# Four of the filling matmul groups at the front of a recurrence-and-convolution kernel take other forms

## The chip, the cores and the metric

The kernel runs on one core of one Trainium2 chip. The metric is the device time of one execution in microseconds (us); less is better. Engines are named as in the profile: PE (TensorE), DVE (VectorE), ACT (ScalarE), POOL (GpSimd), SP (SyncE, which here only issues DMAs). "PEld" is PE's weight loading, which can overlap its matmuls.

## What is computed

Two blocks follow each other on x of shape (4, 6272, 256), batch, sequence, channels. The first is a gated recurrence along the sequence. The second projects its result to three parts, convolves one part circularly along the whole sequence with a long filter, multiplies by the two other parts and projects again:

```python
f = lower_bound + (1 - lower_bound) * sigmoid(f_logit)
h[t] = f[t] * h[t-1] + (1 - f[t]) * x[t]          # y = h, per batch and channel
x1, x2, x3 = split(y @ w_proj, 3)
conv = irfft(rfft(x2, axis=1) * rfft(filter_fft, axis=0), axis=1)
out = (x1 * conv * x3) @ w_out
```

## The kernel before, in words

The sequence of 6272 is treated as 128 x 49, and the long convolution is done by discrete Fourier transforms written as matmuls with tables. The kernel first makes the tables and the filter's spectrum (`prepare`), and then handles the four batches one after the other: the recurrence in 13 chunks of 512 steps (`hgrn`), the projection of the middle part (`phase_p`), the transforms in 16 units (`phase_f1`, `mini`, `unit`), the two other parts (`gate`), and the inverse transform, product and last projection (`phase_o`). Parts of the next batch's recurrence are woven between these.

Nothing of this order is found at run time. Each piece of work is registered as an operation with `op(...)`, numbered as it is registered, and the long string `ORDER` lists number, engine and a PSUM bank for each; `emit` issues them in that order. Each engine works off its own instructions in order and waits where data or a buffer isn't ready. An operation with `take` gets the bank of the list as its argument `p`; `PS` is the whole PSUM, 8 banks of 512 float32 columns on 128 partitions.

The filling groups are the 24 operations "warm" (line 597). Each issues four float16 matmuls of the identity tile with itself, read as float16: 128 rows, 128 weight columns, 256 moving columns. Nobody reads what they write. In the list's order of PE the first eight are the groups 20, 3, 7, 12, 13, 4, 15, 8, all with bank 0, ahead of every other matmul. Two more come later in the front (behind rotation 5), three in the middle of the run, eleven in the tail.

The work of the front, as far as the prediction follows it:

- Loads of the filter: 13 groups of 512 KB (the last is smaller) on SP's queue (line 619) into ten raw buffers. Groups 10, 11 and 12 reuse the first three. Behind them on the same queue come the loads of f_logit and x.
- A cast of each group from the raw buffer into one of two buffers `afs` (lines 284, 296, 289: the helper `copy` on ACT, POOL or DVE). Group 0 is cast on ACT, 1 to 5, 7, 9 and 8 on POOL, 6 on ACT, 10 to 12 on DVE. A cast into a buffer waits for the rotation that read it two groups before.
- A rotation of each group on PE: four matmuls with float32 weights and 256 columns (line 630), into two PSUM banks. Rotation 0 has banks 0 and 1, rotation 1 has 2 and 3, and so on around.
- Two casts of each rotation's result into `f` (ACT, line 284, some on DVE, line 289). ACT's first of these stands behind the sine tables of line 560, which wait for DVE.
- When all groups are there, the filter's two transforms: line 655 and line 673.
- The recurrence: transposes in row pairs, float32, 64 rows each (line 349), the gate (lines 362, 364) and the scan on DVE (line 370).

Later forms that the prediction uses as prices: line 398 and line 714 (projections, float16), line 727 and 790 and 743 (forward transforms), line 832 (inverse, 98 rows), line 895 (64 rows in pairs, float16), line 913 (last projection, float32).

Of the kernel before, what the change touches and what calls it, by code (L numbers as in the profile page):

```python
# [33 lines left out]
NK = 3  # L34
NO = 2
WARM = 24
NEP = 128
UE = 8
NU = NEP // UE
MARGIN = 1.0  # L40
# [20 lines left out]
class Plan:  # L61
# [14 lines left out]
    def op(self, kind, cost, fn, r=(), w=(), dma=0.0, lag=0.0, table=None, take=0, src=None, part=None, margin=0.0):  # L76
        preds = set()
        for t in r:
            if t in self.writer:
                preds.add(self.writer[t])  # L80
        for t in w:
            if t in self.writer:
                preds.add(self.writer[t])
            preds.update(self.readers.get(t, ()))
        me = len(self.ops)
        if src is not None:
            preds.add(src)
            self.ops[src]["users"].append(me)
        self.ops.append(dict(kind=kind, batch=self.batch, cost=cost, fn=fn, preds=preds, dma=dma, lag=lag,
                             table=table, take=take, src=src, part=part, margin=margin, users=[]))  # L90
        for t in r:
            self.readers.setdefault(t, set()).add(me)
        for t in w:
            self.writer[t] = me
            self.readers[t] = set()
        return me
# [98 lines left out]
def kernel(  # L195
# [10 lines left out]
    nc = tc.nc  # L206
# [4 lines left out]
    op = plan.op  # L211

    konst = ctx.enter_context(tc.tile_pool(name="konst", bufs=1))
    iden = konst.tile([128, 128], F32, name="iden")
# [21 lines left out]

    X2 = konst.tile([128, NEP * PW + 16], F16, name="X2")
    xv = X2[:, 0:NEP * PW].rearrange("m (i c) -> m i c", c=PW)

# [17 lines left out]
    PS = psp.tile([128, 8, 512], F32, name="PS")  # L257

    def Wr(kh):

        return [("W", kh, i) for i in range(3)]
# [174 lines left out]
    def prepare(head, tmp):  # L436
# [11 lines left out]
        cols = tmp.tile([128, 16], F32, name="cols")  # L448
# [7 lines left out]
        for i in range(2):  # L456
            small(lambda e, i=i: dve.tensor_copy(rot[:, i * 128:(i + 1) * 128], iden[:]), 128,
                  r=["iden"], w=["rot"], kind="turns")
# [16 lines left out]
        for kh in range(2):  # L475
# [4 lines left out]
               r=["om"] + Wr(1), w=["W13"])  # L480
            for p in range(2):
# [4 lines left out]
                   r=["om"] + Wr(1), w=["W2"])  # L486
# [5 lines left out]
        w = scr[:, 2016:4080].bitcast(F32)  # L492
# [65 lines left out]
        for i, (fn, a, b, c) in enumerate(((args0, 0, 520, 4.2), (args1, 520, 1032, 4.25))):  # L558
# [3 lines left out]
               w=[f"v{i}", "sin"], table="sin")  # L562
# [3 lines left out]
        for i in range(2):  # L566
            small(lambda e, i=i: dve.tensor_scalar(FTr[:, i, 0:TB], in0=tt[i], scalar1=low,
                                                   scalar2=None, op0=AOP.mult), 98, r=["v0"],
                  w=["FTr"], kind="tabs")
            small(lambda e, i=i: pool.tensor_scalar(FTr[:, i, TB:], in0=tt[i][:, 0:Q], scalar1=low,  # L570
                                                    scalar2=None, op0=AOP.mult), 49, r=["v0"],
                  w=["FTs"], e="POOL", kind="tabs")
# [23 lines left out]

        def warm(e, p, i):
            half = iden[:].bitcast(F16)
            for k in range(4):
                nc.tensor.matmul(PS[:, p, 0:256], half[:, 0:128], half, start=True, stop=True)  # L600
        for i in range(WARM):
            op("warm", {"PE": 0.435}, lambda e, p, i=i: warm(e, p, i), r=["iden"], take=1)

        f2 = [pool_.tile([128, NEP // 2 * PF + 16], F32R, name=f"f2{p}")
              for p, pool_ in enumerate((head, tmp))]

        def gaps(e):
            for f in f2:
                pool.tensor_copy(f[:, 0:NEP // 2 * PF].rearrange("m (i c) -> m i c", c=PF)[:, :, Q:64],
                                 iden[:, 0:15].unsqueeze(1).broadcast_to([128, NEP // 2, 15]))  # L610
                pool.tensor_copy(f[:, NEP // 2 * PF:], iden[:, 0:16])
# [4 lines left out]
        for g, r0 in enumerate(range(0, Q, 4)):  # L616
# [9 lines left out]
               r=et, w=[("af", g % 2, 0), ("af", g % 2, 1)])  # L626
# [6 lines left out]
            for p in range(2):  # L633
# [4 lines left out]
                   r=["f2e"], w=[("f2", g, p)], src=rt)  # L638
        op("pad", {"POOL": 2.0}, lambda e: nc.gpsimd.memset(
            X2[:, 0:NEP * PW].rearrange("m (i c) -> m i c", c=PW)[:, :, Q:64], 0.0),  # L640
           w=[("raw", i) for i in range(7)] + [("x2", g) for g in range(NX2)] + ["Hm"])
# [6 lines left out]
        for u in range(NU):  # L648
            af = afs[:, u % 2]
            for h in range(2):  # L650

                def first(e, pb, f=f2[u // 8], j=u % 8 * UE + h * 4):
                    pa = PS[:, pb:pb + 2].rearrange("m a (i c) -> m (a i) c", c=256)
                    for i in range(4):
# [3 lines left out]
                        r=[("f2", g, u // 8) for g in range(13)] + ["D1r", "f2e"],  # L658
                        w=[("FF1", u, h)], take=2)
# [6 lines left out]
                r=[("af", u % 2, 0), ("af", u % 2, 1)],  # L666
                w=["mX"], e="POOL", kind="mX")

            def second(e, pb, af=af):
                for r in range(2):  # L670
                    for e2 in range(2):
# [4 lines left out]
                      r=[("af", u % 2, 0), ("af", u % 2, 1), "FTr", "FTs"], w=[("FF2", u)], take=2)  # L676
# [3 lines left out]
               r=rt, w=ht[u % 2], src=f2nd)  # L680
            for i, (p0, n, to) in enumerate(((0, M, 0), (M - TB, 64, M)) if u % 2 else ()):
                op("hst", {"SP": 0.36}, lambda e, pair=pair, u=u, p0=p0, n=n, to=to: nc.sync.dma_start(
                    H[u // 2][:, to:to + n].rearrange("j r k -> r j k"), pair[p0:p0 + n]),
                   r=ht[0] + ht[1], w=[("H", u - 1, i), ("H", u, i)], dma=0.77 if i else 1.2, lag=1.7)

        def last(e, pb):
# [11 lines left out]
           w=["Hm"], src=lst)  # L698
# [231 lines left out]
    with tc.manual_schedule():  # L930
        scopes = [ctx.enter_context(ExitStack()) for _ in range(2)]
        prepare(*(c.enter_context(tc.tile_pool(name=f"tmp{i}", bufs=1, side=side))
                  for i, (c, side) in enumerate(zip(scopes, ("right", "left")))))
        for i, t in enumerate(more_t):
# [62 lines left out]
```

## Time and profile before

| | |
|---|---|
| median of 3 runs | 457.7 us (456.73 to 458.09) |
| profiled execution, from its first to its last instruction (span) | 455.6 us |
| median less span | 2.1 us |
| mean granted clock of TensorE over the span | 0.989 |
| instructions | 14635 |
| moved by DMA | 120.74 MB, mean 265 GB/s |

The profiled execution has no time of its own besides its span; the span leaves out the little that lies ahead of the first and behind the last instruction. In the rows that follow, a start and a length are given in us, then the engine, the line of the kernel, the operation, what it writes and reads, and how many like it were merged in the row. In brackets stands how long the engine was idle ahead of the row and what released it. Lengths of matmuls overlap, since they are pipelined; what one costs in a dense row is the distance of starts.

### The profile page before, as it was taken

What the parts mean: (1) busy time and instruction counts of PE and PEld (TensorE: products, weight loads), DVE (VectorE), ACT (ScalarE), POOL (GpSimd) and SP (SyncE); (2) the same over time, 40 slices, a digit from 0 to 9 for tenths busy, and PEclk for the clock granted to TensorE, in tenths of its full rate; (3) what the DMA queues carried; (4) which work ended last, traced back from release to release, by engine and by line L of the source; (5) the groups of instructions that cost most, each with busy time, mean ns of one, the idle gap of its engine ahead of it and who ended that gap; (6) DMA issues with size and microseconds to landing.
All of it is one profiled execution on the core that took longest, in us unless ns stands there. A gap on an engine that the chain in (4) does not pass through costs nothing.

```text
span 455.6 us, 14635 instructions
## 1 busy us (share of the span) xinstructions
PE 439.6 (96%) x6009; PEld 348.4 (76%) x6009; DVE 407.4 (89%) x476; ACT 402.3 (88%) x577; POOL 308.8 (68%) x279
## 2 busy tenths in 40 slices
PE   7899999999999999999999999999999999999998
PEld 5687778677767888777668888777778896776797
DVE  8899997799999996999999977999999976989873
ACT  5899999899999987899989998999989858987563
POOL 8888973878899542788995626899994405696400
PEclk9599999999999999999999999999999999999999
DMA  8999999767898985479776896778759721765186
GB/s 326 387 371 345 378 375 361 279 187 233 299 300 282 340 300 237 169 232 374 253 264 219 285 315 272 237 250 303 261 177 317 301 95 46 248 187 185 47 321 246
DMA packets 44434, 120.74 MB, mean 265 GB/s; under 512 B 4304, under 2 KB 7632, under 8 KB 44368
## 3 DMA queue, kind: packets, MB, share of 16 engines
q1 hardware_dynamic: 44368, 119.82, 74.5%
q8 instruction: 47, 0.77, 0.7%
q14 instruction: 19, 0.16, 0.1%
HBM read 86.12 MB, written 31.98 MB: 259 GB/s over the span
## 4 chain that ended last, share of the span: by engine, by line
PE 72%; DVE 11%; ACT 9%; issue 4%; DMA 3%; POOL 1%; SPq 0%; ACTq 0%; DVEq 0%; POOLq 0%
PE PS L398 17%; PE PS L714 9%; PE PS L832 9%; PE PS L913 8%; PE PS L790 7%; DVE HA L370 7%; PE PS L727 6%; PE PS L349 6%; PE PS L895 4%; ACT fTs L362 2%; DMA X<-in_moe_filter_fft_dram 2%; PE PS L600 2%; ACT HA L284 2%; DVE ys L901 1%; ACT X L284 1%
## 5 line engine op out<-in xcount | busy, mean ns | idle before, releaser
L337 POOL TENSOR_TENSOR XT<-XT,FL 128x1024 f32<-128x1024 f32 (+1 forms) x49 | 109.9, 2247 | 55.7 <-ACT FL L335 38.5
L370 DVE TENSOR_TENSOR_SCAN HA<-fTs,HA,PS 128x512 f16<-128x512 f32 (+1 forms) x96 | 112.7, 1202 | 2.0 <-ACT fTs L362 1.1
L398 PE MATMUL PS<-HA,W 128*128 128x490 f16 (+1 forms) x416 | 100.2, 367 | 0.3 <-ACT Th L284 0.2
L822 POOL TENSOR_TENSOR PP<-HA,Hu 98x1008 f16<-98x1008 f16 x42 | 88.0, 2106 | 5.6 <-ACT HA L284 2.6
L284 ACT CAST HA<-PS 128x1024 f16<-128x1024 f32 (+1 forms) x101 | 81.2, 831 | 3.3 <-POOL PP L822 0.8
L901 DVE TENSOR_TENSOR ys<-PS,zt 128x1024 fp32r<-128x1024 f32 (+1 forms) x52 | 58.3, 1151 | 14.0 <-PE PS L895 10.3
L813 DVE TENSOR_TENSOR PP<-PS,Hu 98x1008 f16<-98x1008 f32 x54 | 63.6, 1199 | 1.5 <-PE PS L790 0.7
L362 ACT ACTIVATE fTs<-PS,nomc 128x512 f32<-128x512 f32 (+1 forms) x90 | 59.5, 680 | 4.5 <-PE PS L349 4.2
L398 PEld LDWEIGHTS <-W 128*128 128x128 f16 x416 | 35.3, 97 | 30.2 <-issue 2.9
L428 POOL TENSOR_TENSOR zt<-XS 128x490 f16<-128x490 f32 (+1 forms) x26 | 31.8, 1223 | 39.0 <-DVE ys L901 27.4
L913 PE MATMUL PS<-Wo,ys 128*128 128x256 f32 x392 | 57.5, 293 | 0.4 <-DVE ys L901 0.3
L286 ACT ACTIVATE XS<-PS 128x490 f32<-128x490 f32 (+1 forms) x88 | 51.0, 590 | 6.8 <-DVE zt L419 2.6
L832 PEld LDWEIGHTS <-PP 98*128 98x128 f16 x1024 | 49.2, 98 | 10.1 <-POOL PP L795 1.3
L284 ACT CAST Th<-PS 128x784 f16<-128x784 f32 x63 | 52.0, 828 | 3.4 <-PE PS L832 2.7
L913 PEld LDWEIGHTS PS<-Wo,ys 128*128 128x128 f32 x392 | 49.6, 188 | 4.5 <-DVE ys L901 1.2
L832 PE MATMUL PS<-VA,PP 98*128 98x98 f16 x512 | 52.1, 207 | 0.2 <-POOL PP L795 0.2
L832 PE MATMUL PS<-VB,PP 98*128 98x98 f16 x512 | 51.8, 207 | 0.0
L419 DVE TENSOR_TENSOR zt<-PS,XS 128x490 f16<-128x490 f32 (+1 forms) x78 | 49.2, 648 | 2.7 <-ACT XS L286 0.8
L335 ACT ACTIVATE FL<-FL 128x1024 f32<-128x1024 f32 (+1 forms) x49 | 49.8, 1022 | 0.6 <-DMA FL<-in_f_logit_dram 0.6
L714 PE MATMUL PS<-W,HA 128*128 128x256 f16 x392 | 44.6, 273 | 1.1 <-ACT X L284 1.1
L714 PEld LDWEIGHTS <-HA 128*128 128x128 f16 x392 | 42.9, 142 | 2.0 <-issue 1.3
L349 PE MATMUL PS<-iden,FL 64*128 64x64 f32 x736 | 41.7, 229 | 2.6 <-ACT PP L286 0.6
(119 smaller groups left out, 778.7 us busy)
## 6 DMA issues: line engine op xcount, KB each, us to landing
FL<-in_f_logit_dram SPq DMA_DIRECT2D x45, 512.0 KB, 5.3
XT<-in_x_dram SPq DMA_DIRECT2D x45, 512.0 KB, 6.2
Hu<-H SPq DMA_DIRECT2D x39, 512.0 KB, 4.6
out_dram<-osb SPq DMA_DIRECT2D x24, 512.0 KB, 4.6
out_dram<-PP SPq DMA_DIRECT2D x16, 512.0 KB, 4.8
Hl<-H SPq DMA_DIRECT2D x13, 512.0 KB, 4.7
X<-in_moe_filter_fft_dram SPq DMA_DIRECT2D x9, 512.0 KB, 7.0
out_dram<-HA SPq DMA_DIRECT2D x8, 512.0 KB, 5.7
```

What stands on the lines that cost most here:

```text
L284: nc.scalar.copy(dst, src)
L337: op("u", {"POOL": 0.1 + 0.553 * nb}, lambda e, xt=xt, ft=ft: nc.gpsimd.tensor_tensor(xt, xt, ft, op=AOP.mult), r=[("ft", k)], w=[("xt", k)])
L349: nc.tensor.transpose(bank(pb)[:, at[p] + j:at[p] + hn:nb], src[ps, j, cols], iden[ps, ps])
L362: nc.scalar.activation(fT, sT, AF.Identity, scale=by, bias=1.0)
L370: nc.vector.tensor_tensor_scan(h, fT, bank(pb)[:, 512 - hn:512 + hn], init, op0=AOP.mult, op1=AOP.add),
L398: nc.tensor.matmul(PS[:, p, 0:n], W13[:, kh, js], HA[:, HB[kh] + t0:HB[kh] + t0 + n], start=(kh == 0), stop=(kh == 1))
L714: nc.tensor.matmul(pp[:, r - r0, :], column(HB[kh], q_of(r)), W2[:, kh, :], start=(kh == 0), stop=(kh == 1))
L813: nc.vector.tensor_tensor(pr, px.unsqueeze(1).broadcast_to([TB, 2, UE, 63]), hh(), op=AOP.mult)
L822: nc.gpsimd.tensor_tensor(pr, spec[:, o, :, 1:64].unsqueeze(1).broadcast_to([TB, 2, UE, 63]), hh(), op=AOP.mult)
L832: nc.tensor.matmul(PS[:, ib + o, pr * TB:(pr + 1) * TB], PP[:TB, k, o, n, 2 * pr:2 * pr + 2, :], v[:TB], start=(n == 0), stop=(n == 1))
L901: nc.vector.tensor_tensor(late["ys"][:, yk, :, 0:rn * 128], PS[:, cb:cb + 2, 0:rn * 128], late["zt"][:].rearrange("p k r m -> p k (r m)") ...
L913: nc.tensor.matmul(po[:, i, :], late["ys"][:, yk, kh, i * 128:(i + 1) * 128], Wo[:, kh, :], start=(kh == 0), stop=(kh == 1))
```

## The change

The four filling groups 13, 4, 15 and 8, the last four of the eight ahead of all other matmuls, no longer issue four float16 matmuls of 256 columns each. Group 13 issues 48 float32 transposes of 64 rows in pairs, which write with strides of 4, 1 and 2. Group 4 issues 24 transposes of 32 rows and 16 of 64 rows into 64 columns. Group 15 issues 16 transposes of 128 rows (eight contiguous, eight at stride 4) and 16 float16 matmuls of 64 rows and 64 columns. Group 8 issues 16 float16 matmuls of 64 rows and 128 columns, 8 of 98 rows and 98 columns, and 8 of 128 rows and 128 columns. These four may write to up to four banks from bank 0 on (`take=4`, where `take` only says that a bank is passed). The list `ORDER` and the twenty other groups stay.

```diff
@@ -34,6 +34,7 @@
 WARM = 24
+FORMS = (13, 4, 15, 8)
 NEP = 128
...
         def warm(e, p, i):
             half = iden[:].bitcast(F16)
-            for k in range(4):
-                nc.tensor.matmul(PS[:, p, 0:256], half[:, 0:128], half, start=True, stop=True)
+            lo, hi = slice(0, 64), slice(64, 128)
+
+            def pairs(n, step, tiles=(lo, hi), cols=((0, 128),)):
+                for k in range(n):
+                    for c, (c0, c1) in enumerate(cols):
+                        for j, ps in enumerate(tiles):
+                            w = ps.stop - ps.start
+                            at = w * (k % 2) if step == 1 else k % 2
+                            nc.tensor.transpose(PS[c0:c1, p + j, at:at + w * step:step],
+                                                iden[ps, c0:c1], iden[ps, ps])
+            kind = FORMS.index(i) if i in FORMS else len(FORMS)
+            if kind == 0:
+                pairs(8, 4)
+                pairs(8, 1)
+                pairs(8, 2)
+            elif kind == 1:
+                pairs(6, 1, [slice(32 * j, 32 * j + 32) for j in range(4)])
+                pairs(8, 1, (lo, hi), ((0, 64),))
+            elif kind == 2:
+                for k in range(8):
+                    nc.tensor.transpose(PS[:, p, 128 * (k % 4):128 * (k % 4) + 128], iden[:], iden[:])
+                for k in range(8):
+                    nc.tensor.transpose(PS[:, p, k % 4::4], iden[:], iden[:])
+                for k in range(8):
+                    for j, ps in enumerate((lo, hi)):
+                        nc.tensor.matmul(PS[:, p + j, 0:64], half[ps, 0:128], half[ps, 0:64],
+                                         start=True, stop=True)
+            elif kind == 3:
+                for k in range(8):
+                    for j, ps in enumerate((lo, hi)):
+                        nc.tensor.matmul(PS[:, p + j, 0:128], half[ps, 0:128], half[ps, 0:128],
+                                         start=True, stop=True)
+                for k in range(8):
+                    nc.tensor.matmul(PS[:, p, 0:98], half[:98, 0:128], half[:98, 0:98], start=True, stop=True)
+                for k in range(8):
+                    nc.tensor.matmul(PS[:, p, 0:128], half[:, 0:128], half[:, 0:128], start=True, stop=True)
+            else:
+                for k in range(4):
+                    nc.tensor.matmul(PS[:, p, 0:256], half[:, 0:128], half, start=True, stop=True)
         for i in range(WARM):
-            op("warm", {"PE": 0.435}, lambda e, p, i=i: warm(e, p, i), r=["iden"], take=1)
+            op("warm", {"PE": 0.435}, lambda e, p, i=i: warm(e, p, i), r=["iden"], take=4 if i in FORMS else 1)
```

## The prediction

> **What bounds the kernel now.** I read the page's first two parts first: which engine is full, and where it isn't.
>
> ```profile
> PE 439.6 (96%) x6009; PEld 348.4 (76%) x6009; DVE 407.4 (89%) x476; ACT 402.3 (88%) x577; POOL 308.8 (68%) x279
> PEclk9599999999999999999999999999999999999999
> ```
>
> TensorE is busy for 96% of the span, and its clock is low in one slice of forty only, the second (11.4 to 22.8 us). The four changed groups lie just ahead of it, so the argument belongs to the front. Second, the front cut into stretches of 3.41 us, with the granted clock (columns: busy time and instructions of PE, PEld, DVE, ACT, POOL, then clock, DMA share, GB/s), and the stage behind it:
>
> ```profile
> 4.47:7.88 3.41, 3.27 (x27) 2.65 (x25) 3.31 (x4) 2.33 (x2) 3.24 (x6) 1.00 1.02 417
> 7.88:11.30 3.42, 1.96 (x12) 1.55 (x12) 3.32 (x13) 2.52 (x5) 2.90 (x4) 1.00 1.03 413
> 11.30:14.71 3.41, 2.91 (x14) 2.08 (x13) 3.21 (x8) 3.41 (x8) 2.01 (x2) 0.50 1.03 411
> 18.12:21.53 3.41, 3.41 (x15) 3.01 (x14) 2.85 (x5) 2.05 (x5) 3.41 (x8) 0.50 0.95 343
> ...
> 28.00:60.00 32.00, 30.11 (x428) 24.68 (x428) 31.83 (x35) 31.95 (x49) 29.13 (x31) 1.00 0.98 357
> ```
>
> ```profile
> 21.54:24.95 3.41, 2.64 (x18) 1.00 1.03 422
> ```
>
> The last row has PE alone. The clock falls to half at 11.30, behind a stretch in which PE was busy for 1.96 of 3.42 us, and comes back at 21.5, behind a full one. From 28 to 60 us DVE is busy for 31.83 of 32.00: there the scans set the pace, later PE does. Neither has room to win back time lost ahead of it. Third, PE in order of time (start, length, line, names, count, idle before and releaser), with the four POOL rows that feed it and the first two ACT rows behind it:
>
> ```profile
> 1.36 5.17 PE L600 MATMUL PS<-iden 128*128 128x256 f16 x32 [1.36 <-POOL iden masks.py:199]
> 4.73 1.80 PE L600 MATMUL PS<-iden 128*128 128x256 f16 x15
> 6.28 1.50 PE L630 MATMUL PS<-afs,rot 128*128 128x256 f32 x8
> 7.16 1.04 POOL L296 CAST afs<-X 128x1024 fp32r<-128x1024 f32 x1 [0.17 <-PE PS L630]
> 8.26 0.74 PE L630 MATMUL PS<-afs,rot 128*128 128x256 f32 x4 [0.48 <-POOL afs L296]
> 8.44 2.33 POOL L296 CAST afs<-X 128x1024 fp32r<-128x1024 f32 x2 [0.23 <-DMA X<-in_moe_filter_fft_dram]
> 8.79 0.64 ACT L560 ACTIVATE PP<-PP 128x520 f32<-128x520 f32 x1 [1.95 <-DVE PP L519]
> 9.33 5.49 ACT L284 CAST f<-PS 128x512 fp32r<-128x512 f32 x10
> 10.99 1.14 POOL L296 CAST afs<-X 128x1024 fp32r<-128x1024 f32 x1 [0.23 <-DMA X<-in_moe_filter_fft_dram]
> 12.19 1.23 PE L630 MATMUL PS<-afs,rot 128*128 128x256 f32 x4 [0.50 <-POOL afs L296]
> 13.54 1.41 POOL L296 CAST afs<-Hu 128x1024 fp32r<-128x1024 f32 x1 [1.40 <-PE PS L630]
> 15.00 2.07 PE L630 MATMUL PS<-afs,rot 128*128 128x256 f32 x8
> 22.82 2.94 PE L655 MATMUL PS<-D1r,f 128*128 128x256 f32 x20 [0.77 <-ACT f L284]
> ```
>
> Eight filling groups run from 1.36 to 6.28; 17 of their 32 matmuls start by 4.73, 0.20 us apart, the other 15 are 0.10 apart. The clock column says 1.00 from the start, but this spacing says that full speed came at about 4.5. The changed groups are the last four of the eight, from about 4.6. Behind them comes a loop: rotation 0, POOL's cast for rotation 2 (it needs the buffer that rotation 0 reads), rotation 2, and so on to the first DFT (line 655) at 22.82. POOL waits for a DMA at 8.44 and 10.99, 0.23 us each. So the chain of waits first follows the filter's loads, then POOL and PE:
>
> ```profile
> 3.11 7.73 DMA X<-in_moe_filter_fft_dram
> 10.99 1.15 POOL afs L296
> 12.19 1.23 PE PS L630 x4
> ```
>
> A delay of rotation 0 thus has 0.23 + 0.23 = 0.46 us of cover, and beyond that moves POOL's casts and all that follows.
>
> **The change part by part.** Out go 16 matmuls (groups 13, 4, 15 and 8 in that order), 4.6 to 6.28: 1.7 us. In come 152 instructions on PE with as many weight loads. What one costs in a dense row comes from the nearest shapes, by the distance of starts, since lengths overlap:
>
> ```profile
> 53.22 1.35 PE L349 MATMUL PS<-iden,XS 64*128 64x64 f32 x32
> 54.37 1.20 PE L673 MATMUL PS<-afs,FTr 64*128 64x512 f32 x8
> 428.86 1.98 PE L895 MATMUL PS<-ID,Th 64*128 64x128 f16 x64
> 430.86 2.34 PE L913 MATMUL PS<-Wo,ys 128*128 128x256 f32 x16
> 433.19 0.63 PE L895 MATMUL PS<-ID,Th 64*128 64x128 f16 x16
> 379.03 1.96 PE L727 MATMUL PS<-D,X 128*128 128x128 f16 x32 [0.57 <-ACT X L284]
> 380.92 0.61 PE L790 MATMUL PS<-HA,FT 64*128 64x256 f16 x8
> 382.81 0.27 PE L743 MATMUL PS<-HA,FT 64*128 64x32 f16 x4
> 382.90 1.35 PE L790 MATMUL PS<-HA,FT 64*128 64x256 f16 x16
> 335.08 0.21 PE L832 MATMUL PS<-VA,PP 98*128 98x98 f16 x1
> 336.43 0.21 PE L832 MATMUL PS<-VB,PP 98*128 98x98 f16 x1
> 366.02 6.22 PE L714 MATMUL PS<-W,HA 128*128 128x256 f16 x55
> ```
>
> Per instruction: the kernel's own float32 transposes of 64 rows (54.37 - 53.22) / 32 = 36 ns; float16 with 64 rows and 128 columns 2.00 / 64 = 31; float16 128x128 1.89 / 32 = 59; 64 rows with 32 columns 0.09 / 4 = 23; 98 rows (336.43 - 335.08) / 31 = 44; float32 with full weights (433.19 - 430.86) / 16 = 146; float16 with 256 columns about 6.1 / 55 = 111.
>
> - Group 13: 48 transposes of 64 rows, strides 4, 1 and 2: 48 x 36 = 1.73 us. The kernel's own write at the stride of their block count, so a stride costs nothing extra that I can see.
> - Group 4: 24 transposes of 32 rows, which the trace doesn't show: between 23 (the shortest row) and 36, I take 30: 0.7. Then 16 of 64 rows into 64 columns, not shown either: from 23 to 146, the slowest float32 row; I take 36, the same transposes with twice the columns: 0.6. Sum 1.3, bounds 0.9 and 3.2.
> - Group 15: 16 float32 transposes of 128x128, not shown: between 59 (the same size in float16) and 146. Full float32 weights cost 146 - 111 = 35 ns more than float16 ones at 256 columns, and added to 59 that is 94, the value I take: 1.5; bounds 0.9 and 2.3. Then 16 short float16 matmuls at 31 (23 at least): 0.5. Sum 2.0, bounds 1.3 and 2.8.
> - Group 8: 16 x 31 + 8 x 44 + 8 x 59 = 1.3 us.
>
> Sum 1.73 + 1.3 + 2.0 + 1.3 = 6.4 us (bounds 5.3 and 9.1), where 1.7 stood. I price changes of tiling at nothing: the passage from 64 rows (line 895) to 128 (line 913) at 430.86 is inside the 31 ns.
>
> [...]
>
> **What lies on the path.** PE is free for rotation 0 at 4.6 + 6.4 = 11.0 in place of 6.28, a shift of 4.7 us. The covers: ACT's first cast of a rotation starts at 9.33, held by the table row at 8.79 that waits for DVE, and now waits for rotation 0, so ACT moves by less, some 2.5 us, but POOL's loop moves by the whole: its four casts and the rotations between them, without the two waits for DMA, bring rotation 5 to 11.0 + (12.19 - 6.28) - 0.46 = 16.45 in place of 12.19. That is 4.3 us. ACT, DVE's casts and the DFT wait for later rotations, so 22.82 becomes about 27.1. SP has a queue to watch too: the load of the filter's last group reuses the buffer that POOL's cast at 7.16 reads, so it and the loads of x and f_logit behind it leave later. I price this at nothing: the DMA share is 1.02 to 1.03 up to 14.7, a backlog that covers some microseconds; without that cover, DMA would lose up to the same 4.3 us, beside the shift and not on top of it.
>
> From 28 us on nothing catches up. The execution profiled has a span of 455.6, the median of the runs is 457.7, so about 2.1 us lie around the span and stay. Forecast: 457.7 + 4.3 = **462.0 us**. With the bounds of the forms the delay is 5.3 - 1.7 - 0.46 = 3.1 to 9.1 - 1.7 - 0.46 = 6.9: 460.8 to 464.6. I assume full clock up to 11 and a low one in the rotations behind, as now.
>
> **The rivals.**
>
> *The transposes don't hold the clock (cold).* If they count as idle, the stretch 4.47 to 7.88 holds almost none but them and the clock halves at 7.88. Of the 6.4 us, 3.3 are done by then; 3.1 double, so PE is free at 14.1: delay 14.1 - 6.28 - 0.46 = 7.4, 465.1 us (with the upper bound of the forms 9.1 - 3.3 = 5.8 doubles: 470). Against it speaks a stretch that kept the clock, all of PE first, then line 349 alone:
>
> ```profile
> 42.02:45.43 3.41, 2.75 (x46) 1.00 0.95 346
> 42.02:45.43 3.41, 1.38 (x34) 1.00 0.95 346
> ```
>
> Without the transposes PE was busy there for 2.75 - 1.38 = 1.37 us, less than the 1.96 after which the clock fell at 11.30. So they seem to count for something; whether small tiles alone suffice isn't shown. [...] The row just quoted leans the other way, so I keep the rival at 0.22.
>
> *The clock is kept through the rotations (warm).* PE is now full where 1.96 of 3.42 us were busy, so the fall may come late. Rotation 5 takes 0.74 as at 8.26, not 1.23; the pair at 15.00 takes 1.50 as at 6.28, not 2.07. The rest hides behind casts. That gives back 0.49 + 0.57 = 1.1: 460.9, and with the shortest forms 459.7. Against it: behind rotation 1 POOL's pace leaves PE as idle as it was before 11.30.
>
> *Faster.* The same mechanism at its best: the cold stretch, 11.30 to 21.53, is 10.2 us of PE at half clock; if PE alone set the pace there, a kept clock would save 5.1 us. With the shortest delay, 3.1, that is 2.0 us faster: 455.7. It decides from the point at which the saving exceeds the delay. Against it: in that stretch PE waits for POOL (0.50 at 12.19) and POOL for PE in turn, and ACT and DVE casts follow, so only the 1.1 us above is PE's own.
>
> *The delay is absorbed.* If DMA (share 0.98 from 28 to 60 us) and not DVE sets the scans' stage, its transfers run ahead during the delay and the stage ends as before: 457.7 to 459. Against it: DVE idles for 0.17 us only in 32.
>
> **How the numbers follow.** Main case 0.47; cold 0.22; warm 0.14; absorbed 0.10; faster 0.07. About 0.3% (1.4 us) is what a measurement of this kernel can tell from no change. Faster by more than that: 0.06. Within it: 0.11, the absorbed case and the weak end of the faster one. Slower: 0.83. The range leaves out the absorbed and the faster case and the long tail of the cold one: from 459.2, the warm case with the shortest forms less half a microsecond of scatter between runs, to 467.0, the cold case at 465.1 and a share of its unknown forms.
>
> **What would show it.** Right, step by step: the row of line 630 that starts at 6.28 starts near 11.0; POOL's casts follow without waits for DMA; rotation 5 starts near 16.4; line 655 first runs near 27.1; behind it each engine has its rows about 4.3 us later. The dense rows of transposes are 36 ns apart in group 13. Wrong: the first rotation before 9.9 or after 13.7 (a form's price), a granted clock of 0.50 ahead of it (cold), 1.00 between 12 and 22 us (warm), or rows beyond 60 us that stand where they stood (absorbed).

## The result and the profile after

The changed kernel takes 460.45 us (median of 18 runs, 459.04 to 463.57) beside 458.12 for the kernel before (18 runs, 456.63 to 461.56). The ratio is 1.0056, with a 95% interval of 1.0038 to 1.0073: about 2.6 us slower. The profiled execution has a span of 457.9 us, where before's had 455.6.

The page's first two parts answer to the lines shown of before: the same shares, but the clock isn't low in any slice (ahead of its first rise the column shows full clock too; the last section comes back to that).

```profile
PE 440.8 (96%) x6145; PEld 349.5 (76%) x6145; DVE 404.1 (88%) x476; ACT 402.3 (88%) x577; POOL 307.7 (67%) x279
PEclk9999999999999999999999999999999999999999
```

PE in order of time, with the first ACT and POOL rows behind the changed groups (lines have moved: 608 to 635 are the new forms, 638 the old one, 668 the rotations, 693 the first DFT):

```profile
1.36 3.59 PE L638 MATMUL PS<-iden 128*128 128x256 f16 x16 [1.36 <-POOL iden masks.py:199]
4.88 3.24 PE L608 MATMUL PS<-iden 64*128 64x64 f32 x88
8.05 1.09 PE L620 MATMUL PS<-iden 128*128 128x128 f32 x8
8.98 1.04 PE L622 MATMUL PS<-iden 128*128 128x128 f32 x8
9.95 0.41 PE L625 MATMUL PS<-iden 64*128 64x64 f16 x16
10.19 0.61 PE L630 MATMUL PS<-iden 64*128 64x128 f16 x16
11.51 1.19 PE L668 MATMUL PS<-afs,rot 128*128 128x256 f32 x8
16.42 0.74 PE L668 MATMUL PS<-afs,rot 128*128 128x256 f32 x4 [0.26 <-POOL afs L297]
18.39 1.38 PE L668 MATMUL PS<-afs,rot 128*128 128x256 f32 x8 [0.33 <-POOL afs L297]
25.23 2.94 PE L693 MATMUL PS<-D1r,f 128*128 128x256 f32 x20 [0.94 <-ACT f L285]
...
12.27 5.79 ACT L285 CAST f<-PS 128x512 fp32r<-128x512 f32 x10 [3.61 <-PE PS L668]
12.37 4.00 POOL L297 CAST afs<-X 128x1024 fp32r<-128x1024 f32 x4 [5.39 <-PE PS L668]
```

The forms take 11.51 - 4.88 = 6.6 us, and rotation 0 starts 11.51 - 6.28 = 5.2 us later. Rotation 5, the row at 16.42, is 4.2 us later than before, but the first DFT only 25.23 - 22.82 = 2.4. So the delay came about as forecast, and 2.8 us of it were given back, 1.0 up to rotation 5 and 1.8 behind it. Between 12.37 and 16.37 POOL's four casts run with no wait, 1.0 us each; before, the same four took 1.04, 2.33 for two, and 1.14, 4.5 us in all, and the one behind them 1.41. And the rotations ran at full clock, 1.00 in each of the next rows. The front in stretches (columns as in the prediction):

```profile
7.88:11.30 3.42, 3.42 (x70) 3.06 (x65) 3.11 (x20) 0.64 (x1) 0.00 (x0) 1.00 1.04 418
11.30:14.71 3.41, 2.40 (x22) 2.00 (x20) 1.14 (x4) 2.44 (x5) 2.34 (x3) 1.00 1.02 407
14.71:18.12 3.41, 2.85 (x20) 2.05 (x19) 0.58 (x1) 3.27 (x7) 2.49 (x3) 1.00 1.02 389
18.12:21.53 3.41, 2.31 (x13) 1.79 (x14) 1.74 (x4) 2.70 (x4) 3.30 (x6) 1.00 0.91 344
```

Before, the clock stood at 0.50 from 11.30 to 21.53. DVE, which had been busy for 3.21 us of the stretch from 11.30, is busy for 1.14.

### The profile page after: what moved, and what is told of

It reads as the page before. It is cut to its first block, busy times and chain, and to the rows that moved or that the text cites. A ratio compares the mean times of both kernels' runs of the same rounds, so it can differ in the third digit from the quotient of the medians.

```text
span 457.9 us, 14907 instructions
## 1 busy us (share of the span) xinstructions
PE 440.8 (96%) x6145; PEld 349.5 (76%) x6145; DVE 404.1 (88%) x476; ACT 402.3 (88%) x577; POOL 307.7 (67%) x279
## 4 chain that ended last, share of the span: by engine, by line
PE 67%; DVE 13%; ACT 10%; issue 4%; DMA 1%; POOL 1%; ACTq 0%; DVEq 0%; POOLq 0%; SPq 0%
PE PS L399 17%; PE PS L752 9%; PE PS L870 9%; DVE HA L371 7%; PE PS L828 7%; PE PS L765 6%; PE PS L951 6%; PE PS L350 6%; DVE ys L939 4%; PE PS L933 3%; ACT fTs L363 2%; ACT HA L285 2%; ACT X L285 1%; PE PS L693 1%; DMA FL<-in_f_logit_dram 1%
```

## The experiments

Theory A: the 2.8 us were given back by the clock, which a full PE holds up. Theory B: by what doesn't depend on the clock, that is POOL's casts without DVE beside them, and loads that would have been waited for anyhow. The first four kernels tell these apart. In each run's rows the line numbers are those of its own kernel; the rotations are the rows that read `afs,rot`, the first DFT is the first row that reads `D1r,f`. Diffs leave out what is marked with dots. A profile is one execution of several.

**The same time in the old form.**

```diff
-            for k in range(4):
+            for k in range(16 if i in (13, 4, 15, 8) else 4):
                 nc.tensor.matmul(PS[:, p, 0:256], half[:, 0:128], half, start=True, stop=True)
```

> The four groups stay float16 matmuls of 256 columns, but 16 each in place of 4, which at 0.107 us apart takes about as long as the changed forms took (6.6 us). If only the time on PE ahead of rotation 0 matters, rotation 0 starts at 11.3 to 11.5, the first DFT at about 25.2 and the time is 2 to 2.5 us above before (ratio 1.004 to 1.006), the same as the change. If the transposes as such do something (hold the clock less, or make a later first use cheaper), the two differ by 1 us or more.

Measured: 462.54 us, ratio 1.0099 (1.0071 to 1.0127), about 4.5 us slower. The profiled run:

```profile
1.36 11.42 PE L600 MATMUL PS<-iden 128*128 128x256 f16 x80 [1.36 <-POOL iden masks.py:199]
12.54 1.19 PE L630 MATMUL PS<-afs,rot 128*128 128x256 f32 x8
20.06 1.25 PE L630 MATMUL PS<-afs,rot 128*128 128x256 f32 x8
26.91 2.42 PE L655 MATMUL PS<-D1r,f 128*128 128x256 f32 x10 [0.91 <-ACT f L284]
```

Rotation 0 came at 12.54, not at 11.4: the clock rose near 6.5, 2 us later than in before's profile. Up to there each half microsecond has 4 or 5 matmuls on PE, behind 7.0 it has 7; before's fillers started 0.21 us apart up to 4.5 and 0.11 behind. The clock also fell again in the rotations (mean 0.80 from 14.71 to 18.12, 0.70 from there to 21.53), and once more in the DFT (0.80 from 24.95 to 28.36), of which 10 matmuls took 2.42 us where the change has 20 in 2.94. From rotation 0 to the DFT it took 14.37 us, 0.65 more than in the change. So the match in time failed by 1.0 us, and the run doesn't settle whether the forms matter beside their length.

**The same delay with PE empty.** The four groups issue nothing; DVE writes the rotation's table once more between the last steps of `args1`:

```diff
-            for k in range(4):
+            for k in range(0 if i in (13, 4, 15, 8) else 4):
...
-            fold(520, 1032)
+            a, b = 520, 1032
+            ts(v[:, a:b], in0=w[:, a:b], scalar1=1.0 / S, scalar2=big, op0=AOP.mult, op1=AOP.add)
+            ts(v[:, a:b], in0=v[:, a:b], scalar1=-big, scalar2=float(S), op0=AOP.add, op1=AOP.mult)
+            dve.tensor_copy(rot[:, 0:128], iden[:])
+            dve.tensor_tensor(v[:, a:b], w[:, a:b], v[:, a:b], op=AOP.subtract)
```

> The four groups issue nothing, and rotation 0 waits on DVE instead: DVE writes the rotation's table once more, late in its own table work, so PE idles until about 11.4. Same delay of rotation 0 as in the change, but PE is empty. Theory A (the change gives back 2.8 of 5.2 us because a full PE keeps the clock up in the rotations): the clock falls near 8 and the rotations run at half, 3.5 to 4.5 us above before (ratio 1.008 to 1.010). Theory B (it is given back because POOL's casts and DVE's table work no longer run side by side): the same 2.3 us as the change (1.005).

Measured: 462.95 us, ratio 1.0111 (1.0079 to 1.0143), 5.1 us slower, more than either theory had.

```profile
11.44 2.04 PE L634 MATMUL PS<-afs,rot 128*128 128x256 f32 x8 [6.48 <-DVE rot L560]
13.85 2.21 PE L634 MATMUL PS<-afs,rot 128*128 128x256 f32 x8 [0.37 <-POOL afs L296]
19.89 1.42 PE L634 MATMUL PS<-afs,rot 128*128 128x256 f32 x8
26.93 2.28 PE L659 MATMUL PS<-D1r,f 128*128 128x256 f32 x10 [0.92 <-ACT f L284]
```

Rotation 0 starts at 11.44, as in the change. Two rotations take 2.04 where the change, at full clock, has 1.19 (at 11.51), and the first DFT is at 26.93 in place of 25.23. So at the same delay a full PE is worth 1.7 us at the DFT, in these two executions. The DFT itself then ran slow as well (10 matmuls in 2.28 us, mean clock 0.83 from 24.95 to 28.36), which the 1.7 leaves out. This speaks for theory A; but here, with a slow clock until about 20 (eight fillers at 18.31 took 1.93 us, in the change 1.05), (22.82 - 6.28) - (26.93 - 11.44) = 1.05 us between rotation 0 and the DFT was given back too, and for that part theory B stays.

**No groups at all.** The first edit of the last diff alone.

> The four groups issue nothing, so PE is free at 4.6 and rotation 0 starts when its cast is there, at 5.6 rather than 6.28. The loads still set POOL's casts at 8.44 and 10.99, so nothing is won by that: within 0.3 us of before (ratio 1.000). If the clock falls one stretch earlier, near 8, rotations 2 to 4 run at half and up to 0.5 us is lost (1.001).

Measured: 460.15 us (12 runs), ratio 1.0044 (1.0020 to 1.0069): 2.0 us slower, a miss. The profiled run has its first DFT early, at 22.11, and then loses it:

```profile
22.11 4.13 PE L655 MATMUL PS<-D1r,f 128*128 128x256 f32 x20 [0.92 <-ACT f L284]
```

```profile
22.08:25.50 3.42, 3.39 (x16) 3.39 (x17) 1.81 (x3) 2.54 (x3) 1.93 (x3) 0.50 1.03 418
```

The clock fell at the start of the DFT, whose 20 matmuls took 4.13 us in place of 2.94. The groups of before thus are worth something; in this execution it is the clock that shows it, for the other runs it isn't shown.

**Fillers where PE waits.** The front of before, with fillers ahead of the rotations:

```diff
                 pr = PS[:, pb:pb + 2].rearrange("m a (r e) -> m (a r) e", e=256)
+                half = iden[:].bitcast(F16)
+                for k in range(0 if r0 < 8 else 4 if r0 < 24 else 3):
+                    nc.tensor.matmul(PS[:, pb, 0:256], half[:, 0:128], half, start=True, stop=True)
                 for r in range(r0, r0 + rn):
```

> The front of before, with 4 filling matmuls (float16, 256 columns) ahead of each of the rotations 2 to 5 and 3 ahead of each from 6 on, into the banks that the rotation is about to write, where PE waits for a cast anyhow. Theory A: the clock stays up from 4.5 on without a delay, 1 to 2 us faster than before (ratio 0.996 to 0.998), the first DFT at 21 to 22. Theory B: POOL and DVE run side by side as before, so no change (1.000); if the fillers get in the way, up to 0.5 us slower.

Measured: 457.15 us (12 runs), ratio 0.9988 (0.9962 to 1.0014): not clear of no change. This run is the key to theory B. First PE, then DVE:

```profile
6.31 1.47 PE L633 MATMUL PS<-afs,rot 128*128 128x256 f32 x8
14.43 0.71 PE L633 MATMUL PS<-afs,rot 128*128 128x256 f32 x4
22.69 2.93 PE L658 MATMUL PS<-D1r,f 128*128 128x256 f32 x20 [0.47 <-ACT f L284]
```

```profile
20.24 0.73 DVE L289 CAST afs<-X 128x1024 fp32r<-128x1024 f32 x1 [1.62 <-DMA X<-in_moe_filter_fft_dram]
```

The clock stayed up (1.00 in every stretch from 4.47 to 31.77) and rotation 0 came at 6.31, yet the DFT starts at 22.69, as in before. DVE waited 1.62 us for the load of group 10. So in this execution, without a delay, the filter's loads hold the end of the front, and they would cover a part of a delay.

**Half and twice the forms.** Each count in the four groups halved (`pairs(4, 4)`, `range(4)` and so on), and doubled.

> The change with every count of the four groups halved, so PE is free for rotation 0 at about 8.2 in place of 11.5 (6.28 before). Theory: the delay of 1.9 us is covered, by 0.5 us of waits for the filter's loads at the start of POOL's casts and by the loads of the last groups, which land near 19 to 20 us whatever PE does; the first DFT at 22 to 23 and the time within 0.7 us of before (ratio 0.999 to 1.002). Rival (no cover beyond the 0.46 us of the prediction and no gain from the clock): half the change's shift or more, 1.2 to 1.5 us slower (1.003).

Measured: 458.65 us (11 runs), ratio 1.0012 (0.9991 to 1.0033): as the theory has it, though the rival's 1.003 isn't excluded. In the profiled run the clock rose late: its 44 transposes took 2.30 us (4.89 to 7.19), where the first ballast run further down has 88 in 2.72. Rotation 0 came at 9.04 in place of 8.2. In the rotations the clock was down again: one took 0.74 us at 12.16 and 1.23 at 14.79, and two took 1.19 at 9.04 and 2.06 at 17.40. Its first DFT didn't come at 22 to 23:

```profile
9.04 1.19 PE L668 MATMUL PS<-afs,rot 128*128 128x256 f32 x8
24.68 2.93 PE L693 MATMUL PS<-D1r,f 128*128 128x256 f32 x20 [0.90 <-ACT f L285]
```

Of the shift of 9.04 - 6.28 = 2.8 us, 1.9 reached the DFT in this execution (24.68 in place of 22.82), and its span is 457.4 us, 1.8 above before's. So the median is the theory's, but the profile doesn't bear out that such a delay is covered; the low clock in the rotations may be why, which isn't shown.

> The change with every count doubled, rotation 0 at about 18.1. Theory: past the change's point nothing more is covered, so each further microsecond goes to the end: 6.6 more than the change's 2.3, 8.5 to 9.5 us slower than before (ratio 1.0185 to 1.021), the legs from rotation 0 to the first DFT 13.7 us long as in the change. Rival (the loads set the pace still, or the delay is absorbed later): 5 us or less (1.011).

Measured: 465.81 us, ratio 1.0165 (1.0137 to 1.0193), 7.5 us slower; less than the 8.5 to 9.5 expected. The forms took 12.4 us and not 13.2, which is 0.8 us of what is missing; the rest is within the interval.

```profile
17.27 1.19 PE L668 MATMUL PS<-afs,rot 128*128 128x256 f32 x8
24.15 1.37 PE L668 MATMUL PS<-afs,rot 128*128 128x256 f32 x8 [0.33 <-POOL afs L297]
30.97 2.21 PE L693 MATMUL PS<-D1r,f 128*128 128x256 f32 x15 [0.91 <-ACT f L285]
```

From rotation 0 to the DFT it is 13.70 us, in the change 13.72. So past the change's point nothing more is covered: rotation 0 is 5.8 us later than in the change, the DFT 5.7, and the span 463.5 - 457.9 = 5.6 longer.

**Nothing but transposes.** In the changed kernel, all four kinds replaced by one:

```diff
-            if kind == 0:
-                pairs(8, 4)
...
+            if kind < 4:
+                pairs(23, 4)
```

> The four groups issue nothing but float32 transposes of 64 rows at stride 4, 184 of them, about the same 6.6 us as the change's mixture; no float16 matmul stands between 4.9 and rotation 0. If transposes hold the clock as matmuls do, the granted clock stays 1.00 ahead of rotation 0, rotations start 1.0 us apart behind it, and the time is the change's, 2 to 3 us above before (ratio 1.005 to 1.006). If they count as idle, the clock halves at about 8, PE is free later and rotations run 1.2 us apart: 4.5 us above before or more (1.010).

Measured: 461.29 us (7 runs), ratio 1.0049 (1.0017 to 1.0082), as the change. The stretches here are cut where the clock changes in this run:

```profile
4.61:8.02 3.41, 3.41 (x104) 3.24 (x104) 3.31 (x6) 2.33 (x2) 2.37 (x4) 1.00 1.03 419
8.02:10.75 2.73, 2.73 (x91) 2.66 (x85) 2.46 (x18) 0.64 (x1) 0.00 (x0) 1.00 1.03 416
10.75:14.85 4.10, 2.73 (x21) 2.11 (x17) 4.07 (x5) 3.05 (x6) 3.22 (x4) 1.00 1.02 408
14.85:18.26 3.41, 3.41 (x15) 2.83 (x16) 1.20 (x3) 3.18 (x6) 2.01 (x3) 0.50 1.03 391
```

Rotation 0 came at 10.75, 0.8 us earlier than in the change; the low stretch behind it took that back, and the first DFT came at 25.17.

From 4.78 to 10.75 PE did transposes alone, and the clock stayed up; it fell at 14.85, behind rotations. With no groups at all it had fallen at 8.4 (mean 0.93 from 8.0 to 8.5), behind a stretch with PE busy for 1.5 us of 3.41. The 184 transposes here are 32 ns apart on the average (10.75 - 4.78 = 5.97 us). In the run with the doubled forms PE did nothing but transposes from 4.89 to 10.58, 176 of them and also 32 ns apart; the change's first ones are 53 ns apart up to its clock's rise at 6.0 and 31 behind it. So these transposes, float32 of 64 rows as the kernel's `nc.tensor.transpose` issues them, held the clock in this execution (the trace lists them as matmuls).

**DVE ballast beside POOL's casts.** In the changed kernel, six multiplications on DVE behind its table work:

```diff
-        small(lambda e: dve.tensor_copy(
-            D1r[:], v[:, 0:128].unsqueeze(1).broadcast_to([128, 2, 128])), 256, r=["v0"], w=["D1r"], kind="tabs")
+
+        def d1r(e):
+            dve.tensor_copy(D1r[:], v[:, 0:128].unsqueeze(1).broadcast_to([128, 2, 128]))
+            dve.memset(fTs[:], 1.0)
+            for _ in range(6):
+                dve.tensor_tensor(fTs[:, 0], fTs[:, 0], fTs[:, 1], op=AOP.mult)
+        small(d1r, 256, r=["v0"], w=["D1r"], kind="tabs")
```

> The change with six more DVE multiplications of 128x512 float32 (two inputs) in the stretch 12.4 to 16.6, in which DVE idles in the change and POOL casts. Theory B for the shorter leg from rotation 0 to 5 (4.9 in place of 5.9 us): POOL's casts take 1.0 us there because DVE is still; with the ballast they take 1.1 to 1.4 us, the leg grows by 0.4 to 0.9 us, and the time with it (ratio against before 1.0065 to 1.0075). Rival: only the waits for DMA were lost from that leg and nothing changes against the change (1.0056).

Measured: 463.68 us, ratio 1.0120 (1.0096 to 1.0145). It missed its aim: the ballast (extra work, that is) started at 15.2 and not at 12.4 and ran over, so that DVE's own casts came late and rotation 9 waited 2.9 us for DVE. What it shows is POOL beside it (in the change these two casts take 1.04 each), then DVE:

```profile
16.93 1.24 POOL L297 CAST afs<-Hu 128x1024 fp32r<-128x1024 f32 x1 [0.93 <-POOL afs L297]
19.67 1.40 POOL L297 CAST afs<-HA 128x1024 fp32r<-128x1024 f32 x1
```

```profile
15.22 6.39 DVE L570 TENSOR_TENSOR fTs<-fTs 128x512 f32<-128x512 f32 x6
```

A shorter ballast, with a fill of one half of the tile and two multiplications of it with itself:

> The ballast again, but two multiplications and a shorter fill, so that DVE is done before its next cast is due at 17.5. Only the leg from rotation 0 to rotation 5 is asked for. If POOL's casts are shorter in the change because DVE is still, they now take 1.1 to 1.5 us where a multiplication runs beside them, and the leg grows from 4.9 by 0.2 to 0.5 us. If not, it stays at 4.9.

One run, 464.06 us. The four casts that took 4.00 us in the change:

```profile
12.66 4.91 POOL L297 CAST afs<-X 128x1024 fp32r<-128x1024 f32 x4 [5.68 <-PE PS L673]
```

```profile
13.02 2.67 DVE L570 TENSOR_TENSOR fTs<-fTs 128x512 f32<-128x512 f32 x2
```

They take 4.91: the rotations that wait for the first three start at 13.75, 15.20 and 16.64, so 1.45 and 1.44 us apart, where the change has 0.99 and 0.98 (13.46, 14.45, 15.43). The two multiplications took 2.67 together, 1.3 each; a two-input subtraction of as many columns, at 11.19 in this run and with POOL still, took 0.69. Rotation 5 follows the last cast at 17.6, so its leg from 11.81 is 5.8 us: 0.9 longer, more than expected. So POOL's casts and DVE's multiplications, side by side, both took longer here than alone.

**Against both kernels.** The fillers once more, and with the loads of x and f_logit held back, so that the filter gets the DMA alone, by one DVE write into the first buffer:

```diff
+            dve.memset(FL[:, 1, 0, 0:1], 0.0)
```

It stands behind the copy to `D1r` (line 564).

> The front with fillers between the rotations, and the loads of f_logit and x held back until DVE is through with its table (about 15.2 in place of 12.1), by one small DVE write into their first buffer. In the run with fillers alone, the first DFT waited for the filter's group 10, which landed at 20.1 beside those loads. Theory (without a delay, the filter's loads set the front): group 10 lands by 19, the first DFT comes at about 22.0 in place of 22.7, and the time falls by 0.5 to 1 us against the fillers alone, ratio 0.996 to 0.998 against before. Rival: f_logit then comes too late for the first sigmoid at 24.3, and the time stays or grows.

> The front of before with fillers between the rotations once more, on the same chip as the kernel that holds back the loads: 0.5 to 1.5 us faster than before (ratio 0.997 to 0.999), by the earlier 0.9988 which was not clear of no change.

Measured: with the loads held back 457.71 us, ratio 0.9976 (0.9953 to 0.9998); fillers alone 457.77, ratio 0.9979 (0.9954 to 1.0004); 12 runs each, and 458.60 for before beside them. The first is clear of no change by a hair, the second isn't, and the two don't differ. So holding the loads back won nothing against the fillers alone, where 0.5 to 1 us was expected. DVE's wait for the filter, first with the loads held back, then without:

```profile
18.94 0.71 DVE L289 CAST afs<-X 128x1024 fp32r<-128x1024 f32 x1 [0.38 <-DMA X<-in_moe_filter_fft_dram]
```

```profile
20.31 0.32 DVE L289 CAST afs<-X 128x256 fp32r<-128x256 f32 x1 [0.33 <-DMA X<-in_moe_filter_fft_dram]
```

Group 10 was there by 19 as expected, but so it was in the other run, where only the last group was waited for, 0.33 us: the wait of 1.62 at 20.24 isn't there in every execution. First DFT at 21.72 and 21.67. Both beat the change, by some 0.8% by the ratios. Their mean granted clock is 1.00 in 11 of 12 runs each, before's beside the experiments in 15 of 63.

## Why the prediction came out as it did

Forecast were 4.3 us slower and a range of 459.2 to 467.0; measured were 2.6 and 460.45. The sign and the mechanism were right, the size was not.

- **The forms.** 6.4 us forecast (the four terms add up to 6.3), 6.6 measured, which is closer than the prices were. In the change's profile the clock was low up to about 6.0: the transposes of group 13 started 53 ns apart up to there, 31 behind. In the first ballast run they started 31 ns apart from 4.86 on (88 in 7.58 - 4.86 = 2.72 us), and the forms took 11.05 - 4.86 = 6.2:

```profile
4.86 2.79 PE L613 MATMUL PS<-iden 64*128 64x64 f32 x88
7.58 1.09 PE L625 MATMUL PS<-iden 128*128 128x128 f32 x8
11.05 1.19 PE L673 MATMUL PS<-afs,rot 128*128 128x256 f32 x8
```

  So the sum was a little high, and the late clock, which the prediction didn't have, made up for it. One by one: groups 13 and 4 took 2.72 us at full clock (3.17 in the change), not 3.0, and the upper bound of 146 ns for each of the 16 transposes into 64 columns, 2.3 us in all, wasn't reached. The 128x128 transposes cost (9.95 - 8.05) / 16 = 119 ns, not 94; the short float16 ones (10.19 - 9.95) / 16 = 15, not 31. The first 16 fillers ended at 4.88, not 4.6, again by the later clock.
- **Rotation 5.** Forecast at 16.45, measured at 16.42. Rotation 0 was 0.5 us later than forecast, and POOL's casts were 0.5 us quicker with DVE still, which I hadn't seen; the two cancel, by luck.
- **The cover of 0.46 us, the term that was too small.** I counted only POOL's two waits for DMA. In the three runs with fillers, at full clock and with little or no delay, rotation 0 to the DFT took 16.4 (6.31 to 22.69) and 15.5 (6.14 to 21.67), with the x loads held back and rotation 0 at 7.50 it took 14.2; with the delay it takes 13.7, doubled or not. So at full clock 1.8 to 2.7 us of a delay are covered: by the waits for the filter's loads, up to the last groups, and by DVE's table work being over when POOL casts. Of the shift of 5.2 us that leaves 2.5 to 3.4, and 2.6 was measured. Rows show 1.3 to 2.6 of this cover: POOL's two waits, 0.46; its four casts, 0.5; DVE's wait for the loads, 0.33 to 1.62. The rest isn't traced to a row.
- **"I assume full clock up to 11 and a low one in the rotations behind, as now."** This failed in the profiled execution; it was the rival "warm", forecast at 460.9. Against an empty PE with the same delay the clock was worth 1.7 us at the DFT. I had priced it at 1.1 by two rows alone; the filling groups between the rotations (1.05 us in the change) gain as well, for before they took:

```profile
13.26 1.89 PE L600 MATMUL PS<-iden 128*128 128x256 f16 x8
```

  That 460.45 lies near 460.9 is in part luck, for over many executions the clock doesn't make the difference between the two kernels. Of before's 63 runs beside the experiments 15 have a mean granted clock of 1.00, and these take 457.6 us on average, where the change's 8 such runs of 18 take 460.1: 2.5 apart. At 0.996 they are 3.0 apart (22 and 6 runs), at 0.993 2.2 (13 and 4). The mean doesn't tell when the clock first rose: the change's profiled run has 1.00, though it rose at 6.0 only. Nor was the clock safe in the change: 10 of its 18 runs have a mean below 1.00. In its profile PE was busy for 2.22 us of the stretch 12.85 to 16.26, and the clock stayed up; with 16 matmuls per group it was 2.15 by the rows in the like stretch, the 3.41 us up to about 16.8, and the clock fell behind it.
- **"From 28 us on nothing catches up."** This held: the DFT came 2.4 us later, and the span is 457.9 - 455.6 = 2.3 longer.
- **SP's queue, priced at nothing.** This held: the first load of f_logit left at 14.29 in place of 12.14, and the first sigmoid, at 26.72 behind its table load, didn't wait for it.
- **The cold rival.** It falls: transposes alone held the clock for 6 us.
- **The faster rival.** Its best case needed PE to set the pace in the cold stretch. The fillers between the rotations gave that clock without a delay, and 0.1 to 0.2% came of it, hardly clear of no change, not 5.1 us: loads and casts set the pace there.
- **The absorbed rival.** It falls: doubling the forms moved the time by 5 us more for 5.8 us of delay.

## What to carry to other kernels

Work that only fills must end before the first real instruction can start; what it delays beyond that is paid at the end, less what waits elsewhere would have covered (2.3 us of the change's 5.2 were paid, and 5.6 of the 5.8 that the doubled forms added). To size that cover, follow every other chain to the place where they meet, here the last loads of the filter, and not only the waits next to the change. To hold the clock, fill in the gaps where PE waits for a cast rather than in one block ahead of them; here the mean granted clock was 1.00 in 30 of 36 runs with such fillers (before: 15 of 63), and that won only some 0.2%, since PE didn't set the pace.

## What the runs showed of the hardware

- The clock was low for 3.41 us with transposes only (14.85 to 18.26) and for 10.24 before (11.30 to 21.54). Its first rise came at 4.5 in before's profile, at 6.0 in the change's and near 6.5 in the run with 16 matmuls per group, though PE did the same up to 4.5. The times of one kernel differ along with its mean clock: before's 15 runs with 1.00 took 457.6 us on average, its 11 runs with 0.989 took 459.3.
- The clock fell behind stretches with PE busy for 1.96 us of 3.42 (before, 7.88 to 11.30), about 1.5 of 3.41 (no groups, up to 8.4) and 2.15 of 3.41 (16 matmuls per group, up to about 16.8). It stayed up behind 2.22 of 3.41 (the change, 12.85 to 16.26), and behind 2.31 with rotations 1.0 us apart (the change, 18.12 to 21.53). Once low, it stayed so before behind 2.91 and 3.04 of 3.41 (up to 14.71 and 18.12) and rose behind 3.41 (18.12 to 21.53). These rows don't say what a fall or a rise needs.
- The clock column can show 1.00 where PE runs slow. In the run with an empty PE it shows 1.00 in every stretch up to 21.53, while two rotations take 2.04 us at 11.44 (in the change 1.19). There the distance of starts tells.
- A float32 transpose of 128x128 cost 119 ns in a row (16 from 8.05 to 9.95), and 16 float16 matmuls of 64 rows and 64 columns 15 ns each (9.95 to 10.19).
- Two DVE multiplications of 512 float32 columns took 2.67 us beside POOL's casts (second ballast run, at 13.02), and a two-input subtraction of as many columns took 0.69 in the change with POOL still (at 11.18). The four casts of POOL there took 4.91 us in place of the change's 4.00.
